# A planned single-core kernel: the bonus vector spread by a product, stores on two queues, token sums unit by unit, and a new plan

## The chip, the cores and the metric

The kernel runs on one core of one Trainium2 chip. The time is device microseconds for one execution. Before the change the median of four runs is 126.28 us (126.03 to 126.58). The engines are named as the profile names them: PE (TensorE products) with its weight loads PEld, DVE (VectorE), ACT (ScalarE), POOL (GpSimd) and SP (SyncE, which here only issues transfers). Each engine executes its own instructions strictly in the order of the program; an instruction that has to wait holds up everything behind it on the same engine. ACT and SP also issue transfers, each on a queue of its own; the transfers themselves run on 16 shared DMA engines.

## The reference

Two stages in a row. The first is a linear attention with a decay for each channel and a bonus vector `u` for the present token (4 batches, 8 heads, 768 tokens, 48 channels a head):

```python
for t in range(S):
    cur = einsum('bhd,bhe->bhde', u[None] * kt, vt)
    y[:, :, t] = einsum('bhd,bhde->bhe', rt, state + cur)
    state = wt[:, :, :, None] * state + einsum('bhd,bhe->bhde', kt, vt)
```

The heads' outputs side by side make `x` (4 x 768 x 384). The second stage mixes tokens with weights made from the tokens themselves:

```python
W_tok = scale * einsum('bsd,btd->bst', x @ w_q, x @ w_k)
mixed = einsum('bst,btd->bsd', W_tok, x)
out = maximum(mixed, 0) @ w_out
```

All inputs and the output are float32. The kernel never forms `W_tok`: it takes the sums over tokens of k times x first (64 x 384 a batch, called T), and multiplies q with them.

## The kernel before, in words

The 768 tokens of a batch are worked in three units of 256 tokens, so there are twelve units, 0 to 11. A unit's tensors w, k, r and v are loaded with one transfer each of 384 KB (`load`, line 141) into tiles of which three of each kind exist, so a load also waits until an earlier unit has given its tile back. Then, each step a small function:

- ACT takes the logarithm of the decay (`log`), PE sums it along the tokens by products with triangular matrices (`sums`), ACT makes exponentials of the sums (`expk`, `expr`, `decay`), and POOL and DVE scale k and r with them (`kdec`, `rdec`).
- PE transposes both into `psT` (`trR`), DVE copies them to `RKT` (`evT`), PE makes the token-by-token matrices A in two halves (`amat`), DVE masks them (`mask`).
- POOL multiplies k with the spread bonus vector and then with r (`uk1`, `uk2`), DVE sums each head (`red`), POOL scales v with it (`vd`).
- PE makes the state's update and adds the state of before (`state`, `stadd`), DVE scales it (`stev`). The output Y is put together on PE from three parts (`ymat`, `yst`, `yd`) and copied to X (`yev`), transposed (`xtr`, `xev`), and multiplied with the weights of q and k (`qkmat`, `qkev`).

When a batch's three units are through, its tail follows: `tmat` (twelve products into T), `tev`, three `mix` with two copies with relu each (`mixev`), six `fin` products with copies to `osb` (`finev`), and three stores of two transfers each (`store`).

What is peculiar is the order. There is no loop over engines' work: every step of every unit gets a planned time, `start[n]` plus an offset from one of the lists `steps`, `first` (unit 0) and `last` (unit 11), and for the batches `bstart[b]` plus an offset from `bsteps` or `blast`; loads have `lstart[n]`. All are sorted by that time, and the program is written out in the sorted order:

```python
for _, _, fn in sorted(plan, key=lambda x: x[:2]):
    fn()
```

The planned times are thus only an order, kept on each engine; no engine waits for a clock. Copies that two engines can do are given to ACT (1) or DVE (0) by the tuples `EX` (yev), `ET` (xev), `EQ` (qkev), `EM` (mixev) and `EF` (finev). The functions' `need` only looks up that a step was written out before; waits come from the tiles that an instruction reads or writes.

On SP the order of loads is: the bonus vector (`uload`, line 472, first of all), units 0, 1, 2, the three weight tensors (`wload`), then units 3, 4, 5, 6, 10, 7, 8, 9, 11. All stores are issued on ACT's queue. PE's accumulators are in two pools of PSUM: two large tiles for psT, A, Sn and Y, and four small ones for the rest.

Of the kernel before, what the change touches and what calls it, by code (L numbers as in the profile page):

```python
# [11 lines left out]
F32 = mybir.dt.float32  # L12
# [6 lines left out]
def _rep(ap, axis, n):  # L19
    a = [list(x) for x in ap.ap]  # L20
    a.insert(axis, [0, n])
    return dataclasses.replace(ap, ap=a)
# [3 lines left out]
def kernel(  # L26
# [12 lines left out]
    nc = tc.nc  # L39
    B, H, S, D = r.shape  # L40
    C = 128
    C2 = 2 * C
    HC = C // 2

    EX = (1, 1, 1, 1, 1, 1, 0, 1, 1, 1, 1, 0)
    ET = (1, 1, 1, 0, 1, 0, 1, 1, 0, 0, 1, 0)
    EQ = (1, 1, 1, 1, 1, 0, 1, 0, 1, 1, 0, 0)
    EM = (1, 1, 1, 0, 1, 0, 1, 1, 1, 0, 1, 1, 1, 1, 1, 0, 1, 1, 0, 1, 1, 1, 0, 1)
    EF = (0, 1, 1, 1, 1, 1, 1, 1, 1, 0, 1, 1, 1, 1, 1, 1, 0, 1, 1, 1, 0, 0, 0, 0)
    NCH = S // C  # L50
    NP = H // 2
    NU = S // C2
    NT = B * NU
    D2 = 2 * D
    DM = H * D
    DH = moe_w_q.shape[1]
# [6 lines left out]
    def mm(o, l, rr, start=True, stop=True, trans=False):  # L63
        nc.tensor.matmul(o, l, rr, start=start, stop=stop,  # L64
                         skip_group_check=True, is_transpose=trans)
# [22 lines left out]
    for i in range(NB):  # L88
        for lst, nm in ((LW, "logw"), (RdS, "RdS"), (KdS, "KdS")):
            lst.append(consts.tile([C, 2, NP, C], BF16, name=f"{nm}{i}", tag=f"{nm}{i}"))  # L90

    ubc = consts.tile([C, DM], F32, tag="ubc")
    wq_sb = consts.tile([128, NK, DH], BF16, tag="wq")
    wk_sb = consts.tile([128, NK, DH], BF16, tag="wk")
# [17 lines left out]
    def mtile(shape, dtype, name):  # L112
        return ps.tile(shape, dtype, name=name, tag="m", bufs=4)
# [15 lines left out]
    def at(t, fn):  # L129
        plan.append((t, len(plan), fn))  # L130
# [3 lines left out]
    T = {}  # L134

    def need(*keys):
        for key in keys:
            T[key]
# [239 lines left out]
        copy(EQ[n], T["qk", b][:, m], T["qkp", n])  # L378


    def tmat(b):
        need(*[("qkev", NU * b + m) for m in range(NU)])
        Tps = mtile([2 * DH, DM], F32, "Tps")
        for c in range(NCH):
            for q in range(2):
                mm(Tps[ds(q * DH, DH)], T["qk", b][:, c // 2, c % 2], T["X", b][:, c],
                   start=(c == 0), stop=(c == NCH - 1))
        T["Tps", b] = Tps

    def tev(b):  # L390
        T["Tsb", b] = msb.tile([2 * DH, DM], BF16, name="Tsb", tag="Tsb")
        nc.scalar.copy(T["Tsb", b], T["Tps", b])
        T["mixT", b] = msb.tile([128, NK, 2, NU * C], BF16, name="mixT", tag="mixT")
# [30 lines left out]
    def store(b, g):  # L424
        need(("finev", b, 2 * g), ("finev", b, 2 * g + 1))
        for j in range(2):
            nc.scalar.dma_start(
                out=out[b, ds(g * C2, C2), :].rearrange(
                    "(q i j) d -> j i q d", q=2, j=2)[j],
                in_=T["osb", b, g][ds(j * HC, HC)])  # L430
# [7 lines left out]
    nc.vector.memset(Q4, 0.0)  # L438
    nc.vector.memset(Q4[0:HC, :, 0], 1.0)
    nc.vector.memset(Q4[HC:C, :, 1], 1.0)  # L440
    nc.vector.memset(NEG, 0.0)
    nc.vector.memset(NEG[0:64, :, 1], -100.0)
    nc.vector.memset(NEG[64:128, :, 0], -100.0)
# [26 lines left out]
            e.memset(gaps(t), 0.0)  # L470

    def uload():
        nc.sync.dma_start(out=ubc, in_=_rep(u.rearrange("h d -> (h d)"), 0, C))

    def wload():
        T["wl"] = True
# [3 lines left out]
    def wcast():  # L480
# [5 lines left out]


    steps = [
        (-3.91, log, ()),
        (-3.03, uk1, ()),  # L490
        (-0.42, sums, ()),
        (-0.39, expk, ()),
        (-0.39, expr, ()),
        (-0.02, kdec, ()),
        (0.09, uk2, ()),
        (1.44, rdec, ()),
        (1.54, decay, ()),
        (6.05, trR, (1, )),
        (6.21, vcast, ()),
        (6.37, red, ()),  # L500
        (6.46, trR, (0, )),
        (6.82, evT, ()),
        (7.89, amat, (0, )),
        (9.57, mask, (0, )),
        (9.99, amat, (1, )),
        (10.61, mask, (1, )),
        (10.77, vd, ()),
        (11.56, state, ()),
        (11.59, stadd, (0, )),
        (13.28, stev, (0, )),  # L510
        (14.31, stadd, (1, )),
        (14.34, stev, (1, )),
        (14.88, ymat, ()),
        (14.96, yd, ()),
        (15.01, yst, ()),
        (15.04, yev, ()),
        (17.24, xtr, ()),
        (17.46, xev, ()),
        (20.52, qkmat, ()),
        (21.16, qkev, ()),  # L520
    ]
    first = [
        (-0.64, log, ()),
        (-0.1, uk1, ()),
        (3.13, sums, ()),
        (3.16, expk, ()),
        (4.25, expr, ()),
        (4.55, kdec, ()),
        (4.58, trR, (1, )),
        (5.39, decay, ()),  # L530
        (5.42, rdec, ()),
        (6.03, trR, (0, )),
        (6.12, vcast, ()),
        (7.21, uk2, ()),
        (7.68, evT, ()),
        (8.49, amat, (0, )),
        (9.75, amat, (1, )),
        (11.19, mask, (0, )),
        (11.22, mask, (1, )),
        (13.4, red, ()),  # L540
        (13.93, vd, ()),
        (14.27, state, ()),
        (15.2, stadd, (0, )),
        (15.64, stev, (0, )),
        (15.67, stadd, (1, )),
        (15.81, ymat, ()),
        (15.84, yst, ()),
        (15.92, stev, (1, )),
        (15.93, yd, ()),
        (15.96, yev, ()),  # L550
        (17.78, xtr, ()),
        (18.79, xev, ()),
        (21.33, qkmat, ()),
        (24.77, qkev, ()),
    ]
    last = [
        (-9.8, uk1, ()),
        (-5.81, log, ()),
        (-0.72, sums, ()),
        (-0.17, expk, ()),  # L560
        (-0.17, expr, ()),
        (-0.14, rdec, ()),
        (1.08, decay, ()),
        (2.37, kdec, ()),
        (3.03, uk2, ()),
        (5.28, vcast, ()),
        (5.61, trR, (1, )),
        (7.18, trR, (0, )),
        (7.21, evT, ()),
        (9.13, red, ()),  # L570
        (9.46, amat, (0, )),
        (12.13, amat, (1, )),
        (12.53, state, ()),
        (13.0, mask, (0, )),
        (13.03, mask, (1, )),
        (14.03, stadd, (0, )),
        (14.93, stev, (0, )),
        (15.53, vd, ()),
        (16.58, ymat, ()),
        (16.61, yst, ()),  # L580
        (16.78, yd, ()),
        (20.84, yev, ()),
        (20.87, xtr, ()),
        (22.06, xev, ()),
        (22.94, qkmat, ()),
        (23.25, qkev, ()),
        (28.8, stadd, (1, )),
        (28.83, stev, (1, )),
    ]
    bsteps = [  # L590
        (0.1, tmat, ()),
        (0.13, tev, ()),
        (1.53, mix, (0, )),
        (1.56, mixev, (0, 0, )),
        (1.56, mixev, (0, 1, )),
        (2.75, mix, (1, )),
        (2.78, mixev, (1, 0, )),
        (4.39, mixev, (1, 1, )),
        (5.03, mix, (2, )),
        (5.29, mixev, (2, 0, )),  # L600
        (6.71, mixev, (2, 1, )),
        (7.44, fin, (0, )),
        (7.47, finev, (0, )),
        (8.81, fin, (1, )),
        (9.16, finev, (1, )),
        (9.63, fin, (2, )),
        (9.95, finev, (2, )),
        (11.04, store, (0, )),
        (11.22, fin, (3, )),
        (11.25, finev, (3, )),  # L610
        (12.52, fin, (4, )),
        (12.98, store, (1, )),
        (13.86, finev, (4, )),
        (15.62, fin, (5, )),
        (17.37, finev, (5, )),
        (17.85, store, (2, )),
    ]
    blast = [
        (2.2, tmat, ()),
        (4.38, tev, ()),  # L620
        (4.41, mix, (1, )),
        (4.83, mixev, (1, 0, )),
        (5.91, mixev, (1, 1, )),
        (6.39, mix, (0, )),
        (6.42, mixev, (0, 0, )),
        (6.42, mixev, (0, 1, )),
        (6.46, mix, (2, )),
        (6.49, mixev, (2, 0, )),
        (18.94, mixev, (2, 1, )),
        (18.97, fin, (0, )),  # L630
        (19.73, fin, (1, )),
        (20.89, finev, (0, )),
        (20.92, finev, (1, )),
        (21.16, store, (0, )),
        (21.38, fin, (2, )),
        (21.56, fin, (3, )),
        (21.9, fin, (4, )),
        (22.16, finev, (2, )),
        (22.19, finev, (3, )),
        (22.63, fin, (5, )),  # L640
        (23.24, finev, (4, )),
        (23.6, store, (1, )),
        (24.1, finev, (5, )),
        (24.13, store, (2, )),
    ]
    start = [0.09, 8.5, 15.81, 23.33, 31.0, 38.52, 46.04, 53.76, 61.11, 68.83, 76.15, 83.78]
    bstart = [42.24, 64.62, 85.87, 110.04]
    lstart = [-100, -99, -98, 0.02, 5.76, 12.52, 19.58, 22.33, 51.6, 58.19, 19.73, 59.04]
    for n in range(NT):
        for i, (nm, ap) in enumerate((("w", w), ("k", k), ("r", r), ("v", v))):  # L650
            at(lstart[n] + 0.01 * i, lambda n=n, nm=nm, ap=ap: load(n, nm, ap))
# [4 lines left out]
    for b in range(B):  # L656
        for dt, fn, a in (blast if b == B - 1 else bsteps):
            at(bstart[b] + dt, lambda b=b, fn=fn, a=a: fn(b, *a))
    at(-109.467, uload)
    at(-88.27, wload)  # L660
    at(19.02, wcast)
    with tc.manual_schedule():
        for _, _, fn in sorted(plan, key=lambda x: x[:2]):
            fn()
# [30 lines left out]
```

## Time and profile before

| what | us |
|---|---|
| median of four runs | 126.28 |
| the profiled execution's own time | 126.03 |
| its span | 124.1 |
| PE busy | 98.8 |
| DVE busy | 89.4 |
| POOL busy | 84.7 |
| ACT busy | 79.5 |
| first log starts | 6.50 |
| first product of the sums of units 0, 5, 7, 8, 9 | 7.40, 43.60, 60.46, 68.89, 77.55 |
| last copy of osb ends | 118.63 |
| last store's issue ends | 120.56 |

In rows of the timeline the first number is the start, the second the time from the first start to the last end of the merged instructions, then the engine, the line, the operation, the tiles written and read, and, in brackets, how long the engine had been idle before and what ended that. `SPq` and `ACTq` are the queues' issues: such a row's length is the time to issue, not the transfer. In the page's second part each digit is a slice of a fortieth of the span, 3.1 us, in tenths.

### The profile page before, as it was taken

To read this page: it belongs to the slowest core of one execution; us is meant where nothing else is said; L and a number is where in the kernel's file an instruction comes from. 1 tells how busy PE (TensorE), PEld (TensorE's weight loads), DVE (VectorE), ACT (ScalarE), POOL (GpSimd) and SP (SyncE) were. 2 spreads that over 40 slices of the span, in tenths; PEclk is the share of its full clock that TensorE was granted. 3 is DMA by queue.
4 is the path that set the end of the run, shared out by engine and by line. 5 is a ranking of instruction groups with operands and counts; after the bars stand their busy time and mean duration, and the time that the engine had idled before them with its cause. 6 is when DMAs were issued, how large, how long until landed. Compare 5 with 4: busy or idle time off the path is not lost. (4 is left out here: it accounts for less than half of the span.)

```text
span 124.1 us, 4278 instructions
## 1 busy us (share of the span) xinstructions
PE 98.8 (80%) x1820; PEld 64.2 (52%) x1820; DVE 89.4 (72%) x142; ACT 79.5 (64%) x152; POOL 84.7 (68%) x81
## 2 busy tenths in 40 slices
PE   0064949979798998999899979999999999966900
PEld 0032538546575755756647646657576666632500
DVE  6103378889888989799549898996899987743520
ACT  4054944779889875892797639897688659114500
POOL 8837499998899989778389896699984904000000
PEclk9999999999999999999999999999999999999998
DMA  1999999999999999999999998993145000563084
GB/s 50 242 261 263 263 261 265 301 241 243 266 262 255 232 269 255 225 258 254 236 277 315 312 320 213 246 251 86 58 127 132 0 5 3 131 153 102 2 232 146
DMA packets 54739, 24.85 MB, mean 200 GB/s; under 512 B 51136, under 2 KB 54720, under 8 KB 54720
## 3 DMA queue, kind: packets, MB, share of 16 engines
q1 hardware_dynamic: 51264, 19.86, 68.4%
q10 hardware_dynamic: 3456, 4.72, 13.5%
q8 instruction: 14, 0.23, 0.8%
q14 instruction: 5, 0.04, 0.1%
HBM read 19.86 MB, written 4.72 MB: 198 GB/s over the span
## 5 line engine op out<-in xcount | busy, mean ns | idle before, releaser
L239 DVE TENSOR_TENSOR AmB<-A,MASK 128x1024 bf16<-128x1024 f32 x24 | 29.1, 1219 | 2.1 <-PE A L64 2.1
L245 POOL TENSOR_TENSOR uk<-kG,ubc 128x768 f32<-128x768 f32 x12 | 21.8, 1816 | 8.4 <-DMA kG<-in_k_dram 8.4
L202 POOL TENSOR_TENSOR KdS<-kG,em 128x768 bf16<-128x768 f32 x12 | 19.6, 1637 | 6.9 <-ACT em L173 6.9
L252 POOL TENSOR_TENSOR uk<-uk,rG 128x768 f32<-128x768 f32 x12 | 21.7, 1811 | 0.0
L195 DVE TENSOR_TENSOR RdS<-rG,cw 128x384 bf16<-128x384 f32 x24 | 12.2, 551 | 12.3 <-ACT cw L180 12.2
L266 POOL TENSOR_TENSOR Vd<-V,diag 128x768 bf16<-128x768 bf16 x12 | 17.7, 1474 | 3.9 <-DVE diag L259 3.9
L173 ACT ACTIVATE em<-cw,bias 128x384 bf16<-128x384 f32 x24 | 13.0, 579 | 7.8 <-PE cw L64 7.7
L64 PE MATMUL cw<-logw,BI 128*128 128x384 bf16 x36 | 11.4, 374 | 7.9 <-ACT logw L150 7.9
L222 DVE COPY RKT<-psT 128x2048 bf16<-128x2048 bf16 x12 | 14.6, 1218 | 3.6 <-PE psT L64 3.5
L150 ACT ACTIVATE logw<-wG 128x768 bf16<-128x768 f32 x12 | 10.2, 846 | 10.5 <-DMA wG<-in_w_dram 10.5
L64 PEld LDWEIGHTS <-KdS 64*128 64x128 bf16 (+1 forms) x256 | 11.2, 100 | 8.4 <-POOL KdS L202 2.5
L64 PE MATMUL fps<-wout_sb,mixT 128*128 128x384 bf16 x72 | 14.6, 328 | 0.2 <-DVE RdS L195 0.2
L64 PEld LDWEIGHTS <-RKT 48*64 48x64 bf16 (+1 forms) x464 | 10.2, 108 | 6.4 <-issue 4.4
L297 DVE TENSOR_TENSOR SB<-Sn,pt 128x384 bf16<-128x384 f32 x20 | 11.0, 552 | 2.1 <-PE Sn L64 1.4
L180 ACT ACTIVATE cw<-cw,bias 128x384 f32<-128x384 f32 x24 | 12.2, 551 | 0.2
L259 DVE TENSOR_REDUCE diag<-uk 128x16 f32<-128x768 f32 x12 | 11.3, 946 | 0.5 <-POOL uk L252 0.5
L64 PE MATMUL cw<-logw,BS 128*128 128x384 bf16 x36 | 11.3, 371 | 0.0
L125 ACT COPY osb<-fps 128x384 f32<-128x384 f32 x17 | 8.0, 488 | 3.7 <-PE fps L64 3.6
L64 PE MATMUL A<-RKT 48*64 48x128 bf16 x384 | 10.3, 229 | 0.0
L64 PE MATMUL psT<-ID,KdS 128*128 128x128 bf16 x96 | 8.2, 235 | 2.4 <-POOL KdS L202 1.9
L125 ACT CAST X<-Y 128x768 bf16<-128x768 f32 x10 | 8.0, 802 | 3.2 <-PE Y L64 2.7
L206 ACT CAST V<-vG 128x768 bf16<-128x768 f32 x12 | 10.0, 834 | 0.0
(70 smaller groups left out, 161.7 us busy)
## 6 DMA issues: line engine op xcount, KB each, us to landing
wG<-in_w_dram SPq DMA_DIRECT2D x12, 384.0 KB, 6.3
kG<-in_k_dram SPq DMA_DIRECT2D x12, 384.0 KB, 6.3
rG<-in_r_dram SPq DMA_DIRECT2D x12, 384.0 KB, 6.4
vG<-in_v_dram SPq DMA_DIRECT2D x12, 384.0 KB, 6.1
out_dram<-osb ACTq DMA_DIRECT2D x24, 192.0 KB, 3.1
wout_f<-in_moe_w_out_dram SPq DMA_DIRECT2D x1, 576.0 KB, 6.0
ubc<-in_u_dram SPq DMA_DIRECT2D x1, 192.0 KB, 4.2
wq_f<-in_moe_w_q_dram SPq DMA_DIRECT2D x1, 96.0 KB, 6.1
```

The costliest lines, as they stand in the source:

```text
L64: nc.tensor.matmul(o, l, rr, start=start, stop=stop, skip_group_check=True, is_transpose=trans)
L125: (nc.scalar.copy if e else nc.vector.tensor_copy)(o, i)
L173: nc.scalar.activation(em[:, j], T["cw", n, 1 + j][:, 0:DM], ACT.Exp, bias=bias[2 + j], scale=-1.0)
L180: nc.scalar.activation(cw, cw, ACT.Exp, bias=bias[j], scale=1.0)
L195: nc.vector.tensor_tensor(pad(Rd)[:, j], jhd(T["r", n])[:, j], T["cw", n, j][:, 0:DM].rearrange("p (h d) -> p h d", d=D), ALU.mult)
L202: nc.gpsimd.tensor_tensor(pad(T["Kd", n]), jhd(T["k", n]), hd(T["em", n]), ALU.mult)
L222: nc.vector.tensor_copy(RKT, T["psT", n])
L239: nc.vector.tensor_tensor(T["AmB", n][:, js].rearrange("p q h t -> p h q t"), T["A", n, js], _rep(_rep(MASK[:, js], 1, NP), 1, 2), ALU.mult)
L245: nc.gpsimd.tensor_tensor(uk, T["k", n].rearrange("p h (j d) -> p h j d", j=2), _rep(ubc.rearrange("p (h d) -> p h d", d=D), 2, 2), ALU.mult)
L252: nc.gpsimd.tensor_tensor(uk, uk, T["r", n].rearrange("p h (j d) -> p h j d", j=2), ALU.mult)
L259: nc.vector.tensor_reduce(diag.rearrange("p j h -> p h j"), T["uk", n], axis=AX.X, op=ALU.add)
L266: nc.gpsimd.tensor_tensor(Vd, T["V2", n], _rep(T["diag", n], 3, D), ALU.mult)
```

## The change

Four things at once.

The bonus vector is no longer loaded to all 128 partitions by one transfer of 192 KB. Its 384 numbers are loaded once (1.5 KB), and a float32 product with a row of ones spreads them over the partitions, from where DVE copies them to `ubc`. The load stands on SP behind w and k of unit 0; the product (`ucast`) is the first of the plan on PE, its copy the first on DVE.

`tmat` is split in three calls, each for one unit; the plan places the calls of a batch next to each other on PE.

Each of the 24 store transfers goes to ACT's or to SP's queue, by the new tuple `ES`: one of each pair in batch 0, the second of the last pair in batch 1, none in batch 2, and in batch 3 the first, third, fifth and sixth go to SP.

The plan is new throughout: the tuples of engines, the offsets, `start`, `bstart` and `lstart`. On SP the loads now go 0, 1, 2, weights, 3, 4, 6, 5, 7, 10, 8, 9, two of batch 0's stores, 11, and then the other stores that SP has. On POOL, `vd` of a unit stands before `kdec` of the next, where it stood after `uk2` of the next; for units 0 and 1 `vd` of 1 stands before `vd` of 0.

```diff
-    EX = (1, 1, 1, 1, 1, 1, 0, 1, 1, 1, 1, 0)
-    ET = (1, 1, 1, 0, 1, 0, 1, 1, 0, 0, 1, 0)
-    EQ = (1, 1, 1, 1, 1, 0, 1, 0, 1, 1, 0, 0)
-    EM = (1, 1, 1, 0, 1, 0, 1, 1, 1, 0, 1, 1, 1, 1, 1, 0, 1, 1, 0, 1, 1, 1, 0, 1)
-    EF = (0, 1, 1, 1, 1, 1, 1, 1, 1, 0, 1, 1, 1, 1, 1, 1, 0, 1, 1, 1, 0, 0, 0, 0)
+    EX = (1, 1, 1, 1, 1, 1, 1, 1, 1, 1, 1, 0)
+    ET = (1, 1, 1, 1, 0, 0, 0, 0, 0, 1, 1, 0)
+    EQ = (1, 0, 1, 0, 0, 0, 1, 0, 1, 1, 1, 0)
+    EM = (1, 1, 1, 0, 1, 0, 0, 1, 1, 0, 1, 1, 1, 1, 1, 1, 1, 1, 1, 0, 1, 1, 0, 1)
+    EF = (0, 1, 0, 1, 1, 1, 1, 0, 0, 1, 1, 0, 1, 1, 1, 1, 1, 1, 0, 0, 0, 0, 0, 0)
+
+    ES = (1, 0, 0, 1, 0, 1, 1, 1, 1, 1, 1, 0, 1, 1, 1, 1, 1, 1, 0, 1, 0, 1, 0, 0)
...
+    u1 = consts.tile([1, DM], F32, tag="u1")
+    one = consts.tile([1, C], F32, tag="one")
...
-    def tmat(b):
-        need(*[("qkev", NU * b + m) for m in range(NU)])
-        Tps = mtile([2 * DH, DM], F32, "Tps")
-        for c in range(NCH):
+    def tmat(b, m):
+        need(("qkev", NU * b + m))
+        if m == 0:
+            T["Tps", b] = mtile([2 * DH, DM], F32, "Tps")
+        T["tm", b, m] = True
+        for c in (2 * m, 2 * m + 1):
             for q in range(2):
-                mm(Tps[ds(q * DH, DH)], T["qk", b][:, c // 2, c % 2], T["X", b][:, c],
+                mm(T["Tps", b][ds(q * DH, DH)], T["qk", b][:, m, c % 2], T["X", b][:, c],
                    start=(c == 0), stop=(c == NCH - 1))
-        T["Tps", b] = Tps
...
-            nc.scalar.dma_start(
+            (nc.scalar if ES[2 * (b * NU + g) + j] else nc.sync).dma_start(
...
+    nc.vector.memset(one, 1.0)
...
     def uload():
-        nc.sync.dma_start(out=ubc, in_=_rep(u.rearrange("h d -> (h d)"), 0, C))
+        nc.sync.dma_start(out=u1, in_=u.rearrange("h d -> (h d)"))
+
+    def ucast():
+        ups = mtile([C, DM], F32, "ups")
+        mm(ups, one, u1)
+        nc.vector.tensor_copy(ubc, ups)
...
-    start = [0.09, 8.5, 15.81, 23.33, 31.0, 38.52, 46.04, 53.76, 61.11, 68.83, 76.15, 83.78]
-    bstart = [42.24, 64.62, 85.87, 110.04]
-    lstart = [-100, -99, -98, 0.02, 5.76, 12.52, 19.58, 22.33, 51.6, 58.19, 19.73, 59.04]
+    start = [0.42, 8.84, 16.14, 23.73, 31.34, 38.86, 46.52, 54.11, 61.53, 69.25, 76.58, 84.42]
+    bstart = [40.55, 65.17, 85.94, 114.26]
+    lstart = [-100, -99, -98, -11.4, -9.09, 4.54, 0.63, 6.68, 49.1, 51.23, 17.9, 58.9]
...
-    at(-109.467, uload)
-    at(-88.27, wload)
-    at(19.02, wcast)
+    at(-99.985, uload)
+    at(-99.0, ucast)
+    at(-67.84, wload)
+    at(19.23, wcast)
```

The list of a middle unit's steps, as far as POOL and the first steps go:

```diff
     steps = [
-        (-3.91, log, ()),
-        (-3.03, uk1, ()),
-        (-0.42, sums, ()),
-        (-0.39, expk, ()),
-        (-0.39, expr, ()),
-        (-0.02, kdec, ()),
-        (0.09, uk2, ()),
-        (1.44, rdec, ()),
...
-        (10.77, vd, ()),
+        (-3.67, log, ()),
+        (-1.33, uk1, ()),
+        (-0.45, sums, ()),
+        (-0.42, expk, ()),
+        (-0.25, expr, ()),
+        (1.36, kdec, ()),
+        (1.89, rdec, ()),
+        (2.24, decay, ()),
+        (3.56, uk2, ()),
...
+        (6.51, vd, ()),
...
```

and of the last batch's tail, where the order of the mixes changes with the engines of their copies:

```diff
     blast = [
-        (2.2, tmat, ()),
-        (4.38, tev, ()),
-        (4.41, mix, (1, )),
...
-        (6.39, mix, (0, )),
...
-        (6.46, mix, (2, )),
...
+        (12.66, tmat, (0, )),
+        (12.96, tmat, (1, )),
+        (13.44, tmat, (2, )),
+        (13.55, tev, ()),
+        (13.58, mix, (0, )),
+        (14.09, mix, (1, )),
+        (14.09, mix, (2, )),
...
```

## The prediction

> **What bounds the kernel now.** I read the page first, then the queue of loads (SP) in time, the waits, the units' first steps on ScalarE and TensorE, and the end. The page's summary rows:
>
> ```profile
> span 124.1 us, 4278 instructions
> PE 98.8 (80%) x1820; PEld 64.2 (52%) x1820; DVE 89.4 (72%) x142; ACT 79.5 (64%) x152; POOL 84.7 (68%) x81
> PE   0064949979798998999899979999999999966900
> DMA  1999999999999999999999998993145000563084
> ```
>
> The reader is to see two regimes. DMA is at 9 from slice 1 to slice 27 (3 to 84 us): the loads stream without a pause, about 1.5 us for 384 KB. PE is full from about 50 us to 109 us. So up to some point a unit starts when its decay tensor lands, and after it PE's own work sets the pace. The queue of loads in time, the slots of the sixth, seventh, eighth and ninth unit loaded (their first transfer, w):
>
> ```profile
> 33.58 1.25 SPq L145 DMA_DIRECT2D wG<-in_w_dram  x1
> 40.20 1.36 SPq L145 DMA_DIRECT2D wG<-in_w_dram  x1
> 46.28 1.31 SPq L145 DMA_DIRECT2D wG<-in_w_dram  x1
> 52.74 1.26 SPq L145 DMA_DIRECT2D wG<-in_w_dram  x1
> ```
>
> By the plan's sorted times these are units 5, 6, 10 and 7. Unit 10 is loaded before unit 7, and this shows on ScalarE, whose log steps 5, 6 and 7 are
>
> ```profile
> 41.46 0.85 ACT L150 ACTIVATE logw<-wG 128x768 bf16<-128x768 f32 x1
> 46.98 0.84 ACT L150 ACTIVATE logw<-wG 128x768 bf16<-128x768 f32 x1
> 59.56 0.84 ACT L150 ACTIVATE logw<-wG 128x768 bf16<-128x768 f32 x1 [2.85 <-DMA wG<-in_w_dram]
> ```
>
> Only unit 7 waits for its transfer; 52.74 to 59.56 is 6.8 us from issue to use (the page's median to landing is 6.3). TensorE's first product of units 5 and 7:
>
> ```profile
> 43.60 0.34 PE L64 MATMUL cw<-logw,BI 128*128 128x384 bf16 x1
> 60.46 0.32 PE L64 MATMUL cw<-logw,BI 128*128 128x384 bf16 x1 [0.45 <-ACT logw L150]
> ```
>
> PE lost only 0.45 us there, because batch 0's tail filled it. The end:
>
> ```profile
> 111.56 1.21 PE L64 MATMUL Tps<-X,qks 128*64 128x384 bf16 x12
> 111.77 0.42 DVE L125 CAST qks<-qk 128x256 bf16<-128x256 f32 x1 [0.74 <-PE qk L64]
> 116.59 3.97 ACTq L427 DMA_DIRECT2D out_dram<-osb  x6
> 116.63 2.00 DVE L125 COPY osb<-fps 128x384 f32<-128x384 f32 x4 [1.46 <-ACT osb L125]
> ```
>
> Six issues at 0.66 us each sit on one queue; the last copy is over at 118.63, the last issue at 120.56, the span at 124.1.
>
> **The change part by part.** *Head.* Gone from the front of SP: the spread load of u, 192 KB. Stores of rows as long (1536 B) took 13.5% of 16 engines' 124.1 us for 3456 packets, 77.5 ns each; 128 of them over 16 engines are 0.62 us, so every later load lands 0.62 us earlier. Added: a 1.5 KB load behind w and k of unit 0 (k was in use at 8.12; now 7.5), a memset (0.06), a product of 128x384 in fp32 and a copy from PSUM (0.55, as the copies of osb). No fp32 product is in the trace: nearest is the bf16 one of this form at the head, 0.32 start to start (7.67 to 7.99); I take between one and six such, 0.3 to 1.9, and 1.3 because four-byte operands are at least twice the data. TensorE and VectorE now hold this step first: unit 0's products wait for it on PE, so they start at about 7.5 + 1.3 + 0.1 = 8.9 instead of 7.40, and k's decay product on POOL (9.88, behind uk of unit 0 at 8.12) at 9.5 + 1.8 = 11.3, 1.4 late. DVE's first waiting work (10.34) needs unit 0's exponentials anyway. From 13.96 to 28.9 POOL ran without a gap there; the later start shrinks, as uk of unit 1 no longer waits for k, to about 0.6 us on PE by unit 2 (with vd of unit 1 now ahead of vd of unit 0, and state 0 behind vcast 0 and log 2). All of it is covered by what follows: the cover is 3 us.
>
> *Loads 6 before 5, 7 before 10.* Unit 5 now sits in the slot issued at 40.20. With 6.3 us to land and 0.62 gained, w of unit 5 is there at 45.9 (with the least and greatest times to landing, 5.3 and 7.5: 44.9 to 47.1), where log 5 ran at 41.46. Behind log 5 on ScalarE stand qkev 2, vcast 4 and the exponentials of unit 5; on PE everything from the sums of unit 5 on. Those sums start at 45.9 + 0.85 + 0.05 = 46.8 against 43.60: 3.2 us late, and POOL's uk of unit 5 at 47.3 (k, 41.65 + 6.3 - 0.62) against 43.20. In return unit 7 is there at 46.28 + 6.3 - 0.6 = 52.0, 7.5 us before its old landing.
>
> What does PE do with that? From start-to-start times in the dense stretches: sums 1.31, Y 1.28, two A 0.70, transposes of X 0.44, state with its addition 0.84, qk 0.57, psT 0.99: 6.13 a unit; Tps 1.10, a mix 0.27, a fin 0.50. From the sums of 5 to those of 9 are four units, Tps twice, five mixes and six fins: 24.5 + 2.2 + 1.35 + 3.0 = 31.05, less 0.6 for the missing parts of units at a batch's border: 30.45. Before took 77.55 - 43.60 = 33.95, so it lost 3.5 us to gaps. With none the changed kernel is at the sums of 9 at 46.8 + 30.45 = 77.25; with all of before's, at 80.75. Following the new orders step by step with the durations above, the later of engine and operand at each step: PE has the sums of 6 at 54.7 (before 51.82), of 7 at 62.2 (60.46), of 8 at 69.7 (68.89), of 9 at 77.9 (77.55), of 10 at 85.8 (85.58). The only gap of note is the transposes of X of unit 6 behind yev 6, 0.75, which before has as well (0.70). Nothing else is late: uk of unit 7 is on POOL at 60.8 (61.03), as vd is moved ahead of kdec into time in which POOL waited for em (6.9 us in all). What is late next after load 7 is only k of unit 9 (before 76.40 with 0.96 idle, now 75.6). So +0.2 to +0.4; I take **+0.25**. Both ends for the range: -0.3 and +3.2.
>
> *Engine choices and order inside units.* VectorE takes ucast, xev 4, 6, 7, qkev 1, 3, 4 and six copies of osb more, and gives up yev 6 and others; between 64 and 88 us it gains 1.2 us on 21.4 busy of 24: still under PE. After 88 it is relieved (xev 9, qkev 10, a mixev, a finev go to ScalarE). Taken at zero, cover PE; without it up to 1.2 us.
>
> *Token sums unit by unit.* Same 12 products. In every batch the three calls stand next to each other in PE's order, and in the trace the first of them starts at 111.56, before the copy of qk that only the last four need (111.77): the wait was already single. Zero; bounds 0 and the 0.25 us by which the loads idled there.
>
> *Stores.* Eight of 24 go to SP: 8 x 0.62 us leave ScalarE's queue. In batch 0 two of them stand before load 11: 1.3 us for a load in use at 90.29 and landed at 81; the copies were done by 67. Hidden by 8 us. Batch 1's stands behind all loads. In batch 3 SP takes four, ACT two. The copies, now all on VectorE, follow PE's 0.53 a piece from 115.55 to 118.6, as before. Then two issues of 0.62 on SP: 119.9 in place of 120.56, so **-0.6**. It could be less: the last 1.18 MB at the most that a slice shows (320 GB/s) are 3.7 us against 3.97 of issue, a gain of 0.3; at most 0.75.
>
> The Trainium skill (Trainium Kernel Development and Optimization, Key Constraints) says that issuing DMAs from several engines only saves the sequencer's issue time, as all share 16 DMA engines. By it alone the gain is the 0.6 of issue and no bandwidth; the row of six issues in 3.97 us says the same, and a reader of the rule would expect nothing where transfers, not issues, close the run.
>
> *Sum.* +0.25 - 0.6 = -0.35. The profiled execution (126.03, its span 124.1 and 1.9 around it) is 0.25 under the median of the four runs; on the median 126.28 it makes **125.9**.
>
> **Rivals.** *A, the forecast*: unit 5's stall is caught up by unit 9. 125.9, own range 125.1 to 126.6. Chance 0.40.
>
> *B, slower: PE does not catch up.* One mechanism: after the stall all engines start unit 5 together, and the leads that let PE run without gaps have to be built again; if the gaps of the next four units are as large as before's 3.5 us, the sums of 9 are 3.2 late, and after 77.55 before has only some 0.3 us a unit to regain: 126.28 + 3.2 - 0.6 = 128.9. It decides from about 1.7 us of gaps on (126.6). For it: PE was short of work in just these units before. Against: the loads are then ahead. Chance 0.32, mostly 126.6 to 128.9.
>
> The trace bears on a worse form: until 24 us the sums' products follow at 0.32 us, later at 0.16, while the granted clock reads 1.00, so PE starts at half pace. The idle before unit 5's sums will be about 2.5 us. The Trainium skill (TensorE: Matmul & The Clock Gate, Part 1) has PE fall back to half clock after an idle window of some 3.4 us. By the rule 2.5 us keeps the pace; if it fell, an estimate from that page's window is 1.7 us more.
>
> *C, load 5 is no gate, or leads help*: w lands at the low end (44.9), ScalarE is freer by the moved stores, and before's gaps of units 7 to 9 vanish: -1.0 in the middle, 124.7. For it: yev and em waits there were ScalarE's (POOL waited 6.9 us for em). Against: DMA is full, the slot is fixed. Chance 0.16.
>
> *D, the second queue buys nothing*, transfers closing the run: +0.25, 126.5. The landing of 3.5 us after the last issue speaks for some of it. Chance 0.12.
>
> **How the numbers follow.** About 0.3% (0.38 us) is what a measurement tells from no change: faster is under 125.9, slower over 126.66. A lies half under, a third inside and little above (0.27, 0.12, 0.01); B 0.02 inside, 0.30 above; C all under; D 0.07 inside, 0.05 above. Faster 0.43, same 0.21, slower 0.36. The range takes A, C's middle and B to 128.4, where about 0.2 is left out: 124.6 to 128.4.
>
> **What would show it.** Log 5 with an idle of 3 to 5 us put down to the DMA of w near 46, and none before log 7; unit 0's first sums at 8.5 to 9.3; sums of 9 within 0.5 us of 77.55 (B: 79 or later; C: 76.8); pairs of issues on SP and ACT at the end, the last over by 120.0, the span 0.6 shorter after the last copy. It is wrong if log 5 doesn't wait, if PE's products after 47 run at the head's pace, or if SP's stores hold up load 11.

## The result and the profile after

The changed kernel takes 128.93 us (median of 22 runs, 127.03 to 130.94); the kernel before, run beside it, takes 126.44 (32 runs, 125.18 to 127.17). The ratio is 1.0147, 95% interval 1.0112 to 1.0183: slower by 1.5%, clear of noise. Ratios, here and below, leave out executions more than 1.5% above the fastest of their kernel (of the changed kernel 11 of 22 remain, with a median of 128.41), so a ratio is not the quotient of the two medians. The forecast was 125.9 with 124.6 to 128.4, so sign and range are both missed. The mean granted TensorE clock goes along with the time of a run of the changed kernel: 127.0 to 127.4 us at 0.99, 128.2 to 129.8 at 0.96 to 0.97, 129.9 to 130.9 at 0.93 to 0.95, and the profiled execution (130.67, span 128.9) is one of the last, so its sizes are the upper end. Its span is 4.8 us longer than that of before, where the medians differ by 2.5; the sizes below are of the profiled pair unless a median is named.

The page of the changed kernel, its summary, PE's slices and the granted clock:

```profile
span 128.9 us, 4284 instructions
PE 102.2 (79%) x1822; PEld 65.3 (51%) x1822; DVE 91.8 (71%) x150; ACT 77.0 (60%) x146; POOL 85.2 (66%) x81
PE   0094929889797429999999989999999999966900
PEclk9999995999999965799999999999999999999985
DMA  3999999989798989999995999950071400274092
```

PE has a hole in slices 14 and 15 (4 and 2 tenths, 42 to 48 us), and from slice 15 on the clock row reads 6, 5 and 7. (The 5 in slice 7 belongs to the head, where PE still waits for loads.) The queue of loads in time (start, length of the issue), the first transfers of units 6, 5, 7 and 10:

```profile
33.21 1.31 SPq L149 DMA_DIRECT2D wG<-in_w_dram  x1
...
39.70 1.38 SPq L149 DMA_DIRECT2D wG<-in_w_dram  x1
...
46.40 1.35 SPq L149 DMA_DIRECT2D wG<-in_w_dram  x1
...
52.16 1.39 SPq L149 DMA_DIRECT2D wG<-in_w_dram  x1
```

ScalarE's log steps of units 5, 6 and 7 in its timeline:

```profile
46.56 0.84 ACT L154 ACTIVATE logw<-wG 128x768 bf16<-128x768 f32 x1 [5.41 <-DMA wG<-in_w_dram]
...
55.71 0.85 ACT L154 ACTIVATE logw<-wG 128x768 bf16<-128x768 f32 x1
...
63.04 0.85 ACT L154 ACTIVATE logw<-wG 128x768 bf16<-128x768 f32 x1
```

Unit 5, now second in the queue, waits for its transfer and has ScalarE stand for 5.41 us; 6 and 7 find theirs there. TensorE's timeline around it, the last product before the hole and the first products of units 5 and 6:

```profile
42.74 0.62 PE L66 MATMUL psT<-ID,RdS 128*128 128x128 bf16 x8
47.46 0.48 PE L66 MATMUL cw<-logw,BI 128*128 128x384 bf16 x1 [4.10 <-ACT logw L154]
47.73 0.53 PE L66 MATMUL cw<-logw,BS 128*128 128x384 bf16 x1
...
57.63 0.34 PE L66 MATMUL cw<-logw,BI 128*128 128x384 bf16 x1
```

And the engines' busy time in windows around it (length; then PE, PEld, DVE, ACT, POOL busy, with the number of instructions; then the granted clock, the DMA share and GB/s):

```profile
43.00:47.00 4.00, 0.36 (x7) 0.24 (x5) 1.86 (x3) 0.44 (x1) 0.00 (x0) 0.91 1.03 241
47.00:50.00 3.00, 2.54 (x30) 1.25 (x31) 0.00 (x0) 2.51 (x5) 1.98 (x2) 0.50 0.99 240
50.00:53.00 3.00, 3.00 (x58) 1.72 (x52) 1.68 (x3) 2.00 (x4) 3.00 (x3) 0.50 1.25 268
53.00:56.00 3.00, 3.00 (x64) 1.89 (x62) 1.94 (x3) 2.17 (x5) 3.00 (x2) 0.99 1.26 269
```

Two costs can be read. PE idles for 4.10 us, and it is granted half the clock for 6.83 us (46.25 to 53.07 in finer windows), of which it works from 47.46 on: the sums of 6 follow those of 5 after 10.17 us (47.46 to 57.63), where before needed 8.22. Against before, the first sums are late by 3.86 at unit 5 (47.46 and 43.60), by 5.81 at unit 6 (57.63 and 51.82), by 3.8 at units 9 and 10 (81.36 and 77.55, 89.39 and 85.58), by 4.43 at the last batch's token sums (115.99 and 111.56), and the span by 4.8.

The head and the end of the changed kernel, from the timelines of all engines:

```profile
4.50 0.84 ACT L154 ACTIVATE logw<-wG 128x768 bf16<-128x768 f32 x1 [2.48 <-DMA wG<-in_w_dram]
6.16 1.61 PE L66 MATMUL ups<-u,one 1*128 1x384 f32 x2 [6.16 <-DMA u<-in_u_dram]
7.70 0.50 PE L66 MATMUL cw<-logw,BI 128*128 128x384 bf16 x1
...
120.08 2.97 DVE L129 COPY osb<-fps 128x384 f32<-128x384 f32 x6 [0.49 <-PE fps L66]
121.14 3.53 SPq L433 DMA_DIRECT2D out_dram<-osb  x4
121.14 1.67 ACTq L433 DMA_DIRECT2D out_dram<-osb  x2
```

The fp32 product costs 1.54 us up to the sums (6.16 to 7.70). The last issue is over at 124.67, 5.98 us after the last pair of mix products starts (118.69); before it was 6.31 (114.25 to 120.56). From the last issue to the span's end it is 4.2 us in place of 3.5.

### The profile page after: what moved, and what is told of

It reads as the page before. It is cut to its first block, busy times and chain, and to the rows that moved or that the text cites. A ratio compares the mean times of both kernels' runs of the same rounds, so it can differ in the third digit from the quotient of the medians.

```text
span 128.9 us, 4284 instructions
## 1 busy us (share of the span) xinstructions
PE 102.2 (79%) x1822; PEld 65.3 (51%) x1822; DVE 91.8 (71%) x150; ACT 77.0 (60%) x146; POOL 85.2 (66%) x81
## 3 DMA queue, kind: packets, MB, share of 16 engines
HBM read 19.66 MB, written 4.72 MB: 189 GB/s over the span
## 4 chain that ended last, share of the span: by engine, by line
PE 59%; ACT 12%; DMA 9%; POOL 5%; DVE 4%; issue 2%; SPq 1%; ACTq 1%; DVEq 0%; POOLq 0%
PE Y L66 10%; PE fps L66 9%; PE cw L66 9%; PE psT L66 7%; DMA wG<-in_w_dram 5%; PE Sn L66 5%; PE qk L66 4%; PE A L66 4%; PE xt_ps L66 4%; PE Tps L66 4%; DMA u<-in_u_dram 3%; POOL uk L249 3%; ACT X L129 2%; ACT XT L129 2%; PE mps L66 2%
## 5 line engine op out<-in xcount | busy, mean ns | idle before, releaser
L129 ACT CAST X<-Y 128x768 bf16<-128x768 f32 x11 | 8.8, 798 | 3.3 <-PE Y L66 3.2
L129 ACT COPY osb<-fps 128x384 f32<-128x384 f32 x13 | 6.1, 484 | 5.6 <-PE fps L66 2.1
```

The source lines that it names most:

```text
L129: (nc.scalar.copy if e else nc.vector.tensor_copy)(o, i)
```

## The experiments

The theory after the result: the order of the loads is the cause, and it costs twice, by the wait for unit 5 and by the half pace of PE that follows. The rivals: one of the other parts costs the time (the product at the head, the new orders inside the units, the stores on SP), or the wait alone is the cost and the clock only shows it.

**The two loads swapped back, in the changed kernel**

```diff
-    lstart = [-100, -99, -98, -11.4, -9.09, 4.54, 0.63, 6.68, 49.1, 51.23, 17.9, 58.9]
+    lstart = [-100, -99, -98, -11.4, -9.09, 0.63, 4.54, 6.68, 49.1, 51.23, 17.9, 58.9]
```

> The changed kernel with loads 5 and 6 in their natural order again (unit 7 stays before unit 10); nothing else touched. Theory G (the load order is the cause: w of unit 5 lands at about 46.5, PE stands for 4 us and its clock falls back): log 5 runs at about 41.3 without waiting for a transfer, the sums of unit 5 start at 43.4, no unit waits for its load, the granted clock near 46 to 54 us is full, and the time is 124.0 to 125.5, below the kernel before, because unit 7 no longer waits either. Theory O (the new orders inside the units, the engine choices and the end are the cause): the wait of log 5 goes, but the time stays above 127.5.

Measured: 126.21 us (11 runs, 125.38 to 128.02), ratio 0.9996 (0.9969 to 1.0023). The loss of 1.5% is gone, so 6 before 5 is its cause. No gain shows either, against the 124.0 to 125.5 expected. The order still has 10 before 8 and 9, and in the profiled execution (127.84, 1.6 above the median), now that unit 5 is in time, unit 9 isn't (timelines of ScalarE and TensorE):

```profile
73.53 0.84 ACT L154 ACTIVATE logw<-wG 128x768 bf16<-128x768 f32 x1 [2.71 <-DMA wG<-in_w_dram]
...
74.80 0.34 PE L66 MATMUL mps<-qks,Tsb 64*128 64x384 bf16 x2 [1.49 <-ACT Tsb L398]
...
77.98 0.50 PE L66 MATMUL cw<-logw,BI 128*128 128x384 bf16 x1
```

Log 9 holds up the copy of the token sums behind it on ScalarE, PE stands for 1.49 us, and its products (0.50 for one, in place of 0.34) run at half the clock from 75.92 to 79.33. That the place of load 10 costs time in the median too is shown by the run further below that moves it behind 9 as well.

**The new order of loads alone, in the kernel before**

```diff
-    lstart = [-100, -99, -98, 0.02, 5.76, 12.52, 19.58, 22.33, 51.6, 58.19, 19.73, 59.04]
+    lstart = [-100, -99, -98, 0.02, 5.76, 19.58, 12.52, 19.7, 51.6, 58.19, 22.33, 59.04]
```

> The kernel before with only the load order of the changed one (6 before 5, 7 before 10). Theory G: log 5 waits until about 47.2 (0.6 later than in the changed kernel, since the spread load of u is still in front), PE stands for 3 to 4 us, and the time rises to 128 to 130. Theory O: the two moves of loads cancel, since unit 7 gains what unit 5 loses, and the time stays at 126.0 to 126.8.

Measured: 131.54 us (5 runs, 130.22 to 133.94), ratio 1.0368 (1.0318 to 1.0418). The one line costs more alone than the whole change. Its ScalarE and TensorE, units 5 and 6, in the longest of the five executions (133.94):

```profile
48.42 0.84 ACT L150 ACTIVATE logw<-wG 128x768 bf16<-128x768 f32 x1 [6.51 <-DMA wG<-in_w_dram]
...
49.32 0.48 PE L64 MATMUL cw<-logw,BI 128*128 128x384 bf16 x1 [5.31 <-ACT logw L150]
...
61.05 0.34 PE L64 MATMUL cw<-logw,BI 128*128 128x384 bf16 x1
```

The sums of 6 follow after 11.73 us here. So the rest of the change, taken together, is a gain of about 2% on top of this order (1.0147 against 1.0368), not a loss.

**PE kept busy during the wait.** The changed kernel, with 20 more products in front of the sums of unit 5, which then overwrite what these leave in `cw`; what is computed stays the same.

```diff
+            if n == 5 and i == 1:
+                for _ in range(20):
+                    mm(cw[:, 0:DM], BI, wout_sb[:, 0])
```

> The changed kernel with twenty more products of 128x384 (0.16 us each at full pace, 3.3 us) written into the accumulator that the sums of unit 5 overwrite, placed in PE's order right before these sums, that is into the time in which PE waits for log 5. They take nothing from anybody if they end before 47.4. Theory clock (a part of the loss is PE's clock falling back during the idle): the sums of unit 5 still start at 47.3 to 47.6 but follow at 0.16 us a product instead of 0.32, the granted clock there stays full, and the time falls by 1.3 to 2.5 us against the changed kernel, to 126.5 to 127.4. Theory wait alone (the delay is that of the data): no change against the changed kernel's 128.4 or so.

Measured: 127.87 us (5 runs, 127.27 to 128.04), ratio 1.0130 (1.0098 to 1.0162). TensorE's timeline of this run:

```profile
43.54 3.41 PE L66 MATMUL cw<-wout_sb,BI 128*128 128x384 bf16 x20
46.81 0.32 PE L66 MATMUL cw<-logw,BI 128*128 128x384 bf16 x1
...
54.67 0.34 PE L66 MATMUL cw<-logw,BI 128*128 128x384 bf16 x1
```

Its windows, in the columns of above:

```profile
41.00:47.00 6.00, 5.75 (x72) 3.92 (x69) 4.14 (x5) 1.59 (x4) 1.14 (x1) 1.00 1.10 257
47.00:55.00 8.00, 8.00 (x161) 5.22 (x160) 5.49 (x9) 7.58 (x16) 7.67 (x5) 1.00 1.05 254
```

The wait of ScalarE is there (4.41 us, log 5 at 45.91), the clock stays at 1.00, and the sums of 6 come 7.86 us after those of 5, 2.31 less than without the extra products. The median is 1.06 below the changed kernel's, short of the 1.3 to 2.5 expected, and the ratios (1.0130 and 1.0147) lie within each other's intervals: this run shows the pace kept, but doesn't prove a gain in time.

**The same in the kernel before with the new order alone**, 28 products at the same place:

```diff
-    lstart = [-100, -99, -98, 0.02, 5.76, 12.52, 19.58, 22.33, 51.6, 58.19, 19.73, 59.04]
+    lstart = [-100, -99, -98, 0.02, 5.76, 19.58, 12.52, 19.7, 51.6, 58.19, 22.33, 59.04]
...
+            if n == 5 and i == 1:
+                for _ in range(28):
+                    mm(cw[:, 0:DM], BI, wout_sb[:, 0])
```

> The kernel before with the changed load order (131.5 us), and 28 more products into the accumulator that the sums of unit 5 overwrite, in PE's order right before them (4.6 us at full pace, where PE stood for 5.3 us). Theory clock: unit 5's sums still start when log 5 lets them, at 48 to 49.4, but follow at 0.16 us a product, and the time falls by 1.5 to 2.5 us, to 129.0 to 130.0. Theory wait alone: unchanged at 131 to 132.

Measured: 129.34 us (6 runs, 129.07 to 129.69), ratio 1.0292 (1.0252 to 1.0333), against 131.54: every run is below every one without the products. TensorE's timeline:

```profile
43.59 4.72 PE L64 MATMUL cw<-wout_sb,BI 128*128 128x384 bf16 x28
48.15 0.33 PE L64 MATMUL cw<-logw,BI 128*128 128x384 bf16 x1
...
56.36 0.34 PE L64 MATMUL cw<-logw,BI 128*128 128x384 bf16 x1
```

8.21 us from unit to unit in place of 11.73. More work on PE made the kernel faster, by 2.2 us in the medians and by 0.8% in the ratios (1.0368 and 1.0292; the intervals overlap a little, and the two were measured on different chips). So the half pace is a cost of its own beside the wait. In these profiles the wait differs too (log 5 at 46.13 and at 48.42), so not every tenth of the difference is the clock's.

**All stores on ACT's queue, in the changed kernel**

```diff
-    ES = (1, 0, 0, 1, 0, 1, 1, 1, 1, 1, 1, 0, 1, 1, 1, 1, 1, 1, 0, 1, 0, 1, 0, 0)
+    ES = (1,) * 24
```

> The changed kernel with all 24 store transfers on ScalarE's queue again. As predicted, the second queue was worth 0.6 us at the end: the time rises by 0.3 to 0.75 against the changed kernel. Rival (the second queue buys nothing, the transfers close the run, and the pair of last stores on one queue is as late): within 0.25 of the changed kernel. Third: faster, if the stores that stand before load 11 on SP hold something up.

Measured: 128.72 us (5 runs, 126.95 to 130.68), ratio 1.0134 (1.0075 to 1.0192): no difference from the changed kernel, but the interval is too wide to exclude 0.6 us. The profiles are closer: from the last pair of mix products to the end of the span it is 10.28 us here and 10.21 with two queues. The profile of this run (127.75) shows something else as well. Log 5 ran 2 us earlier (44.40), and PE's idle was short:

```profile
45.30 0.32 PE L66 MATMUL cw<-logw,BI 128*128 128x384 bf16 x1 [1.64 <-ACT logw L154]
```

The first product takes 0.32, full pace. But in the windows behind it

```profile
46.00:48.00 2.00, 2.00 (x52) 1.31 (x50) 0.04 (x1) 2.00 (x5) 1.54 (x1) 0.69 1.22 254
48.00:50.00 2.00, 2.00 (x28) 0.97 (x26) 1.84 (x3) 1.08 (x3) 2.00 (x3) 0.50 1.15 268
50.00:52.00 2.00, 2.00 (x48) 1.34 (x44) 0.79 (x2) 1.23 (x3) 2.00 (x2) 0.96 1.05 245
```

the clock falls to 0.50 while PE has no gap any more (0.69 over two us puts the fall at 46.76, 0.96 the return at 50.17), and the sums of 6 come 9.28 us after those of 5 (54.58).

**The loads in the order of use, in the changed kernel** (3 to 11 in turn)

```diff
-    lstart = [-100, -99, -98, -11.4, -9.09, 4.54, 0.63, 6.68, 49.1, 51.23, 17.9, 58.9]
+    lstart = [-100, -99, -98, -11.4, -9.09, 0.63, 4.54, 6.68, 49.1, 51.23, 52.0, 58.9]
```

> The changed kernel with the loads in natural order, 3 to 11 (load 10 now after 9 as well). With 5 first alone, the time came down to that of the kernel before and log 9 was the one that waited (2.7 us at 73.5), since load 10 stands before 8 and 9 and keeps one of three tiles. Theory G: no log after unit 2 waits for a transfer, PE has no idle over 1 us between 24 and 109 us, the granted clock is full from 24 us on, and the time is 123.6 to 125.4, below the kernel before. Theory O: other orders hold it at 126 or more.

Measured: 124.11 us (6 runs, 123.57 to 124.49), ratio 0.9879 (0.9828 to 0.9930). It beats both kernels. Two rows of its page:

```profile
span 122.6 us, 4283 instructions
...
PEclk9999999999999999999999999999999999999995
```

ScalarE's and TensorE's timeline at unit 5:

```profile
41.69 0.85 ACT L154 ACTIVATE logw<-wG 128x768 bf16<-128x768 f32 x1
...
43.84 0.33 PE L66 MATMUL cw<-logw,BI 128*128 128x384 bf16 x1
```

No log but the very first waits for its transfer, and the clock row has no dip before its last slice, where PE has finished.

**The loads in the order of use, in the kernel before**

```diff
-    lstart = [-100, -99, -98, 0.02, 5.76, 12.52, 19.58, 22.33, 51.6, 58.19, 19.73, 59.04]
+    lstart = [-100, -99, -98, 0.02, 5.76, 12.52, 19.58, 22.33, 51.6, 58.19, 58.5, 59.04]
```

> The kernel before with the loads in natural order (10 after 9). Its unit 7 waited 2.85 us on ScalarE, but PE only 0.45 us. If the wait was as well covered as I read it, the time stays within 0.4 us of before (125.8 to 126.5); if ScalarE's and POOL's lateness there cost PE its gaps in units 7 to 9, it falls by 0.8 to 2 us.

Measured: 124.57 us (12 runs, 124.37 to 126.17), ratio 0.9927 (0.9890 to 0.9964). The kernel before, too, paid for an order that isn't that of use. Its sums of 7, 8 and 9 are at 59.48, 67.28 and 75.95 in place of 60.46, 68.89 and 77.55: 0.36 of this is there at unit 6 already (51.46 for 51.82), so the late load of unit 7 had cost some 1.2 us in these profiles, not the 0.45 at the first product.

**The bonus vector by the product alone, in the kernel before**

```diff
-        nc.sync.dma_start(out=ubc, in_=_rep(u.rearrange("h d -> (h d)"), 0, C))
+        nc.sync.dma_start(out=u1, in_=u.rearrange("h d -> (h d)"))
...
+    def ucast():
+        ups = mtile([C, DM], F32, "ups")
+        mm(ups, one, u1)
+        nc.vector.tensor_copy(ubc, ups)
...
-    at(-109.467, uload)
+    at(-99.985, uload)
+    at(-99.0, ucast)
```

> The kernel before with the bonus vector's part of the change alone: 1.5 KB loaded behind w and k of unit 0, the fp32 product first on PE, the copy first on DVE. As predicted it is worth 0.6 us to all later loads and costs unit 0's first products: in the changed kernel they started at 7.70 against 7.40. Covered theory: sums of unit 0 at 7.6 to 7.9, log 7 about 0.6 us earlier than 59.56, the time within 0.5 us of before and rather below (125.5 to 126.3). Rival: the head's delay is carried through PE to the end, 126.4 to 126.9.

Measured: 124.92 us (12 runs, 124.10 to 126.04), ratio 0.9949 (0.9914 to 0.9983). A gain by itself. ScalarE's first log and TensorE's first products:

```profile
4.41 0.84 ACT L152 ACTIVATE logw<-wG 128x768 bf16<-128x768 f32 x1 [2.39 <-DMA wG<-in_w_dram]
...
5.64 1.61 PE L64 MATMUL ups<-u,one 1*128 1x384 f32 x2 [5.64 <-DMA u<-in_u_dram]
7.19 0.50 PE L64 MATMUL cw<-logw,BI 128*128 128x384 bf16 x1
```

The first log is 2.1 us earlier than before (6.50), and the sums of 7 are at 58.97: the earlier loads take away PE's wait at unit 7 without a change of order, though log 7 still waits 1.60 us for its transfer.

**The loads in the order of use, and batch 3's end as it was.** The run with 124.11, with the first two copies of `osb` of batch 3 back on ScalarE and batch 3's stores on ACT's queue:

```diff
-    EF = (0, 1, 0, 1, 1, 1, 1, 0, 0, 1, 1, 0, 1, 1, 1, 1, 1, 1, 0, 0, 0, 0, 0, 0)
-    ES = (1, 0, 0, 1, 0, 1, 1, 1, 1, 1, 1, 0, 1, 1, 1, 1, 1, 1, 0, 1, 0, 1, 0, 0)
+    EF = (0, 1, 0, 1, 1, 1, 1, 0, 0, 1, 1, 0, 1, 1, 1, 1, 1, 1, 1, 1, 0, 0, 0, 0)
+    ES = (1, 0, 0, 1, 0, 1, 1, 1, 1, 1, 1, 0, 1, 1, 1, 1, 1, 1, 1, 1, 1, 1, 1, 1)
```

> The kernel of natural loads with the end of the kernel before: batch 3's six store transfers on ScalarE's queue and its first two copies of osb on ScalarE. If the second queue was worth 0.6 us as predicted, 0.3 to 0.75 slower than natural loads alone. If transfers close the run and the new end is 0.35 us longer from the last mix to the end of the span (10.2 against 9.85 in the two profiles), 0.2 to 0.5 faster. If neither, equal within 0.2.

Measured: 124.14 us (6 runs, 123.86 to 124.86), ratio 0.9897 (0.9842 to 0.9952), equal to 124.11 within noise. From the last pair of mix products to the end of the span the two profiles have 9.82 and, with two queues, 9.85: the new end is worth nothing on an undelayed kernel either.

**The kernel before with the product and the order of use**, its plan otherwise untouched: the edits of the last run but one and of the last but two together.

> The kernel before with two things: natural loads and the bonus vector by the product; its own orders inside the units, engine choices and end stay. Against the kernel of natural loads with the changed plan (0.988 of before): if the new orders and choices are worth nothing, the same ratio within 0.003; if they help, this one stays at 0.990 or above; if they cost (more work on VectorE, the longer end), it goes to 0.985 or below. The two parts alone gave 0.993 and 0.995; if they add up, 0.988.

Measured: 124.48 us (10 runs, 124.03 to 125.81), ratio 0.9922 (0.9882 to 0.9963). The two gains (0.9927 and 0.9949) would add up to 0.988, just below this interval; the repetition below doesn't exclude it (0.9870 to 0.9948). If they don't add up, the likely reason is that both shorten the same wait of unit 7.

**The last two once more, side by side**: the changed kernel with the loads in the order of use (the edit that gave 124.11), and the kernel before with product and order of use (124.48).

> The changed kernel with its loads in the order of use (the loads as in the run e5_natural), now measured on the same chip and against the same runs of the kernel before as the old plan with the same two improvements. The question is what the rest of the new plan is worth: engines, orders inside the units, calls of the token sums, queues of the stores. Theory 1, nothing: in the profiles the sums of unit 10 stand at 83.45 here and at 83.80 with the old plan (0.35 earlier), and from there to the last batch's token sums PE takes 26.61 here against 25.98 (0.63 later), so this kernel should be 0 to 0.3 us slower than e12, ratio to before about 0.992. Theory 2, the new orders are a gain: 0.988 again, 0.4 us or more faster than e12.

> The kernel before with two parts alone, the bonus vector by the product and the loads in the order of use (as in e9_old_plan_natural_product); everything else of the old plan stays. Theory 1: 0.992 of before or lower, equal to e11 or up to 0.3 us faster. Theory 2: 0.4 us or more slower than e11.

Measured: 124.29 us (6 runs, 123.62 to 124.50), ratio 0.9856 (0.9814 to 0.9898), against 125.04 (10 runs, 124.19 to 126.25), ratio 0.9909 (0.9870 to 0.9948). The new plan is ahead in both comparisons, by 0.4 and 0.75 us, though the intervals still overlap. In the profiles of these two the sums of 10 are 1.47 us earlier with the new plan (83.09 and 84.56), and some 0.6 of it is given back behind unit 10. So what is left of the change, above all its engines and orders inside the units, is likelier a gain than nothing, which was my first theory there.

## Why the prediction was wrong

Three terms of the sum failed: +0.25 for the late load of unit 5, −0.6 for the stores, and zero for the orders inside the units.

*Loads 6 before 5: the gate.* Right in kind and place. Log 5 was expected at 45.9; it ran at 46.56, 45.91 and 44.40 in three profiles with this order and the new plan. The sums of 5 were expected at 46.8 and ran at 47.46, 46.81 and 45.30. Log 7 waits for nothing, as expected.

*Loads 6 before 5: "the idle will be about 2.5 us", which keeps the pace.* This step failed, and with it the term of +0.25. The idle was 4.10 in the profiled execution: PE was through with its work at 43.36, 0.9 earlier than I had it, and the transfer landed 0.66 later. And the dismissal was wrong for a short idle as well: after 1.64 us the clock still fell, 1.5 us into the dense work. The Trainium skill (TensorE: Matmul & The Clock Gate, Part 1) names an idle window of some 3.4 us as the condition; here a gap of 1.64 us, with dense work behind it, was followed by 0.50 from 46.76 to 50.17, so an idle shorter than that figure is no assurance and the measurement decides. Its other figure, about as long a busy stretch before the pace is back, fits the 3.41 us of that run, and the changed kernel's profile too: its 6.83 us are twice 3.41, and only in the second half did PE work without a gap. The estimate of 1.7 us more, should the pace fall, is near the 1.42 that the single stretch cost (9.28 from unit to unit for 7.86). The sign of being wrong that the prediction named, products after 47 at the head's pace, came true.

*The following of orders step by step.* Right against the kernel before, once the pace is kept. With the extra products the sums of 6 to 10 are at 54.67, 62.21, 70.07, 78.40 and 86.42, where the working had 54.7, 62.2, 69.7, 77.9 and 85.8. The term of +0.25 measured +0.84 there (86.42 less 85.58), and with the half pace +3.81 (89.39 less 85.58): 2.97 us more, of which 0.65 are the landing (47.46 for 46.81) and 2.31 the clock. But what is regained here is regained against a kernel that itself loses time behind unit 6. Against the same plan with its loads in the order of use, nothing is regained (first products, us):

| sums of unit | 5 | 6 | 8 | 10 | token sums of the last batch |
|---|---|---|---|---|---|
| loads in the order of use | 43.84 | 51.70 | 67.11 | 83.45 | 110.06 |
| 6 before 5, with extra products | +2.97 | +2.97 | +2.96 | +2.97 | +2.97 |
| 6 before 5, one store queue | +1.46 | +2.88 | +2.87 | +2.88 | +2.87 |
| 6 before 5, the changed kernel | +3.62 | +5.93 | +5.92 | +5.94 | +5.93 |

The column of unit 5 is what the wait leaves, what unit 6 adds is the half pace (none with the extra products), and both are carried to the last batch in full. (The two orders in the kernel before do the same: 6.08 late at unit 5, 9.60 from unit 6 on.) B's price, 128.9, is the median measured, but that is luck: B had gaps while the engines build up their leads again, and with the pace kept none showed (7.86 from unit 5 to unit 6, as with the loads in the order of use). "A worse form", written under B, was a part of the cause.

*Engine choices and order inside units: "taken at zero, cover PE".* Wrong by 0.62 in this stage. From the sums of 10 to the last batch's token sums, PE takes 26.60 or 26.61 in all seven profiles with the changed plan, and 25.98 or 25.99 in all seven with the old one, at a clock of 1.00. PE's busy time there is 25.41 in the changed kernel and 24.83 before, so most of the loss is not idle: some products follow the one ahead of them more slowly. One place is 0.27 us behind a pair of mix products (102.68 to 103.22, where before has 98.59 to 98.86); the rest I haven't placed.

*Stores: −0.6.* Failed. The issues were over 0.33 us earlier, and the transfers then closed the run 4.2 us after the last issue in place of 3.5; counted from the last mix products the end is 0.36 later (10.21 and 9.85). With one queue it is 10.28, and with the loads in the order of use 9.85 with two queues and 9.82 with one: the queues make no difference, and the 0.36 are not theirs. Rival D said so, and the rule of the Trainium skill weighed there (Trainium Kernel Development and Optimization, Key Constraints: issuing from several engines only saves issue time) held. The lone figure of 3.5 us from issue to end should have decided: this span ends in transfers, and issues that ended sooner did not end it sooner.

*Head.* Price of the product right (1.3 expected, 1.54), and the calls by unit look worth zero, as expected, though no run has them alone: the products of `Tps` again start 0.21 us ahead of the copy (115.99 and 116.20). Wrong were the 0.62 us for the spread load (worked out from 3456 packets taken as 1536 B each, though 4.72 MB over them are 1366 B): the first log came 2.0 us earlier (4.50), the u of 1.5 KB was there at 6.16 and not with k at 7.5, and the sums of 0 started at 7.70 in place of 8.9. Of the 2.0 us, 1.85 are left at the load of unit 3 (19.06 for 20.91), and only 0.4 to 0.5 at the slots of units 6 and 5. This misses on the side of a gain, and by itself the part gains 0.5%.

*The sum*, for the profiled pair: catch-up +0.84, landing and clock +2.97, orders behind unit 10 +0.62, the last mix +0.01, the end +0.36: +4.8, as measured, where the forecast had +0.25 and −0.6. In the profile with one store queue (127.75 us, span 125.9) it is +0.75 up to unit 10, +0.62 behind it and +0.43 at the end: +1.8. There the stores' term is the furthest off (by 1.0), ahead of the orders (0.6) and the catch-up (0.5); in the profiled execution of the changed kernel it is the wait and the clock. *Shown* by runs: that the order of loads causes the loss (undone, it is gone; alone, it makes it), and that the second queue is worth nothing. That the half pace is a part of the loss the traces show; by the ratios, the runs with extra products are 0.2% below those without in the changed kernel, which is within noise, and 0.8% in the kernel before. *Open*: why w of unit 5 lands up to 2 us apart from one execution to the next (its issue is at 38.48 to 39.70, and log 5 runs 5.92 to 6.96 later), where the lead of 2 us of the loads goes between units 3 and 5, and what makes the 0.62 and the 0.36.

## What to carry to other kernels

Where the transfers run without a pause, first lay the order of the loads beside the order of their use: the place by which unit 5 was moved back cost a slot (33.21 to 39.70, 6.5 us here), and a unit moved forward gains only if it was waiting. A wait of PE can be paid twice, once as idle and once as half pace (3.41 us or a multiple of it here), and ahead of a stretch that PE fills without gaps it is not made up later; so a wait sized from start-to-start times at full pace is the lower end only. A test with harmless extra products during the wait tells the two apart. Count time saved on issues at the end of a run only where the copies or issues, and not the transfers, end last.

## What was not expected of the hardware

An idle of 1.64 us on PE, followed by products at full pace, led to half the clock 1.5 us later and for 3.41 us, without any further gap; 1.49 us in another run did the same from 75.92 to 79.33. The stretches at half clock last 3.41 us (one store queue), 6.83 (the changed kernel) and 10.24 (the kernel before with the new order), that is one, two and three times the same length. In the changed kernel they begin and end on one grid of that length: 22.35, 46.25 and 53.07 lie 1, 8 and 10 steps of 3.413 us behind 18.94, where the stretch at the head begins. If the clock changes only at such steps, the place of a short idle between two of them decides whether it costs the clock; no run tests that. Extra work on PE (4.72 us of products that nobody reads) made a kernel faster, 129.34 for 131.54 us. And one spread load of 192 KB in front of the queue held the first decay tensor up by 2.0 us, three times what its bytes come to at the stores' rate per packet.
